# Lent PSUM banks for the first chunks, identity products for the prior state, fewer weight pieces, another end, and an order read from a table

## The chip, the cores and the metric

The kernel runs on one core of a Trainium2 chip. The metric is device time in microseconds (us) of one execution, median of three runs. TensorE (PE) multiplies matrices, VectorE (DVE), ScalarE (ACT) and GpSimd (POOL) do elementwise work, SyncE (SP) issues most transfers. PSUM is the memory that PE writes its products to; SBUF is the other on-chip memory.

## The reference

A linear recurrence over 768 steps feeds two feed-forward layers. Cut to what matters:

```python
# r, k, v, w, a, b: [4, 8, 768, 40]; state: [4, 8, 40, 40]
for t in range(768):
    y[:, :, t] = einsum('bhd,bhde->bhe', r_t, state)
    Sa = einsum('bhde,bhe->bhd', state, a_t)
    state = state * w_t[..., None, :] - einsum('bhd,bhe->bhde', Sa, b_t) + einsum('bhd,bhe->bhde', v_t, k_t)
x = y as [3072, 320]                       # tokens x model
x = (relu(x @ w_in1) ** 2) @ w_out1        # w_in 320x2048, w_out 2048x320
h = x @ w_in2
return (h * cos(h)) @ w_out2               # [3072, 320]
```

The four weight matrices arrive as float64, which the kernel reads as pairs of 32-bit integers and turns into float32 itself.

## The kernel before, in words

**The recurrence** is cut into 12 chunks of 64 steps, and its 32 heads into 16 pairs, worked on in 4 groups of 4 pairs. For each chunk `decay` makes running products of w (`lam`, forwards, and a backward scan) with two scans per group on DVE; the scans need a row that is 1.0 at each head's start and 0.0 elsewhere, which stands in the constants `kc` in SBUF (`K_SC`). Two tensors of a chunk, `cin` and `at`, are multiplied with the decays. A solve by 32x32 blocks follows, and then for each group a short chain: `pq` and `pp` from the state, `px`, `pu`, and last `py`, the products that hold the chunk's outputs and the next state's new part. The prior state's part of the outputs is copied to a tile `sz` and added to `py` afterwards on DVE, and the state `MT` is added likewise. The PSUM tiles of these chains come from a ring named `att` with 3 buffers.

**The weights.** Each of 16 column blocks f of a layer has 704 columns (384 of w_in, 320 of w_out). To convert one, ACT makes `u` and `w` from the integers (clamp), DVE works out the bits with two TENSOR_SCALAR and one SCALAR_TENSOR_TENSOR on `u`, POOL adds, and then ACT copies the high half to `ws` while DVE or POOL subtracts it, so that `ws` holds a high and a low part (`split`). Of layer 1, the first `EARLY` blocks are converted by `first`, each in two parts of 384 and 320 columns; the others in the pieces that `PIECES` lists, mixed into the recurrence. Layer 2's blocks 0 to 7 are converted in pieces as well and written back to memory (`w2f`); blocks 8 to 15 are done whole by `Weights.late`, in tiles `wr`, after the recurrence.

**The feed-forward layers** work on blocks of 512 tokens, one column block f a step: 8 matmuls make `h` from the high and low halves of the input (`xh`, `xl`), the activation is made in halves `gh` and `gl`, and 8 matmuls (`po`, layer 1) or 12 (`pt`, layer 2) apply w_out. `h` and `po0`, `po1`, `po2` have PSUM banks of their own. A block of layer 1 needs the outputs of two chunks.

**What sets the order.** Up to the last chunk all operations are first put in a `Book`, with a kind: recurrence, weights, or layer 1. `Book.arrange` then puts them in order greedily, by rank, costs, `BONUS` and the shifts in `PRIORITY`, and chooses the engine of those that may run on two. The rest (the end of layer 1 with `late` woven in by slots, and all of layer 2) is issued in the order of the code. In the profile, line 1058 is the Book's and line 313 the direct part's.

Of the kernel before, what the change touches and what calls it, by code (L numbers as in the profile page):

```python
# [29 lines left out]
EARLY = 8  # L30
# [10 lines left out]
PIECES = ((0, 256), (256, 128), (384, 160), (544, 160))  # L41
# [8 lines left out]
K_ME, K_MO, K_ID, K_RS, K_ONE, K_LIM, K_QT, K_LOW = 0, 104, 208, 248, 249, 250, 251, 252  # L50
# [83 lines left out]
def f32_of_bits(bits):  # L134
# [14 lines left out]
    {'m': 1287429.0, 'y': 1504832.0, ('w', 0): 338963.0, ('w', 1): 299763.0, 'evict': 3771576.0, 'wait': 0.0, ('w', 2): -2016099},  # L149
    {'m': -914107.0, 'cfg': 166353.0, 'stay': 1197706.0})  # L150
# [168 lines left out]
class Nc:  # L319
# [10 lines left out]
    (('c', 0), 'Ls'): -5,  # L330
    (('c', 0), 'M0d'): -19,
    (('c', 0), 'MT0'): 92,
    (('c', 0), 'MT1'): 50,
    (('c', 0), 'MT2'): 48,
    (('c', 0), 'MT3'): 66,
    (('c', 0), 'Ts0'): -4,
    (('c', 0), 'Ts1'): -6,
    (('c', 0), 'at'): 36,
    (('c', 0), 'cin'): -2,
    (('c', 0), 'ga'): -179,  # L340
    (('c', 0), 'kc'): -2,
    (('c', 0), 'l21'): -192,
    (('c', 0), 'lam0'): 169,
    (('c', 0), 'lam2'): -170,
    (('c', 0), 'lent'): 42,
    (('c', 0), 'pm'): -56,
    (('c', 0), 'pn'): 251,
    (('c', 0), 'pp'): -1,
    (('c', 0), 'pt'): -120,
    (('c', 0), 'pu'): -2,  # L350
    (('c', 0), 'pw'): 1,
    (('c', 0), 'px'): -19,
    (('c', 0), 'py'): -68,
    (('c', 0), 'rv'): 1,
    (('c', 0), 't11'): -5,
    (('c', 0), 'tcomp'): -54,
    (('c', 0), 'tt'): -21,
    (('c', 0), 'ttmp'): 38,
    (('c', 0), 'xsb'): -284,
    (('c', 0), 'yt'): -4,  # L360
    (('c', 1), 'Ls'): 55,
    (('c', 1), 'M0d'): -62,
    (('c', 1), 'MT0'): -6,
    (('c', 1), 'MT1'): -19,
    (('c', 1), 'MT2'): 21,
    (('c', 1), 'MT3'): -14,
    (('c', 1), 'ga'): -121,
    (('c', 1), 'kc'): 81,
    (('c', 1), 'l21'): 37,
    (('c', 1), 'lam1'): -4,  # L370
    (('c', 1), 'lent'): -2,
    (('c', 1), 'mov'): -5,
    (('c', 1), 'pgt'): -17,
    (('c', 1), 'pn'): 123,
    (('c', 1), 'pp'): -93,
    (('c', 1), 'pq'): 38,
    (('c', 1), 'pt'): 7,
    (('c', 1), 'pu'): 84,
    (('c', 1), 'pw'): -22,
    (('c', 1), 'px'): 160,  # L380
    (('c', 1), 'py'): -13,
    (('c', 1), 'rv'): -42,
    (('c', 1), 'sz'): 6,
    (('c', 1), 'tcomp'): -72,
    (('c', 1), 'tt'): -10,
    (('c', 1), 'ttmp'): -347,
    (('c', 1), 'xsb'): 3,
    (('c', 10), 'L'): -21,
    (('c', 10), 'M0d'): 115,
# [12 lines left out]
    (('c', 10), 'pgt'): 100,
    (('c', 10), 'pm'): 2,
    (('c', 10), 'pp'): 11,
    (('c', 10), 'pq'): -2,
    (('c', 10), 'pt'): -28,
    (('c', 10), 'pu'): 87,
    (('c', 10), 'pw'): -22,
    (('c', 10), 'px'): -21,
    (('c', 10), 'py'): 98,  # L410
    (('c', 10), 'rv'): 178,
    (('c', 10), 'sz'): 19,
    (('c', 10), 't11'): -37,
    (('c', 10), 'tcomp'): 43,
    (('c', 10), 'tt'): 2,
    (('c', 10), 'ttmp'): 32,
    (('c', 10), 'xsb'): 32,
    (('c', 10), 'yt'): 123,
    (('c', 11), 'L'): -5,
    (('c', 11), 'Ls'): 156,  # L420
    (('c', 11), 'Tw'): -17,
    (('c', 11), 'at'): -125,
    (('c', 11), 'cin'): 135,
    (('c', 11), 'ga'): -9,
    (('c', 11), 'kc'): -58,
    (('c', 11), 'l21'): -65,
    (('c', 11), 'lam2'): 55,
    (('c', 11), 'mov'): 15,
    (('c', 11), 'pgt'): -37,
    (('c', 11), 'pp'): 51,  # L430
    (('c', 11), 'pq'): -21,
    (('c', 11), 'pt'): -85,
    (('c', 11), 'pu'): -8,
    (('c', 11), 'pw'): 48,
    (('c', 11), 'px'): 43,
    (('c', 11), 'py'): 49,
    (('c', 11), 'rv'): -107,
    (('c', 11), 'sz'): -11,
    (('c', 11), 't11'): -12,
    (('c', 11), 'tcomp'): 10,  # L440
    (('c', 11), 'tt'): -58,
    (('c', 11), 'ttmp'): 162,
    (('c', 11), 'xsb'): -209,
    (('c', 11), 'yt'): 68,
    (('c', 2), 'Ls'): -12,
    (('c', 2), 'M0d'): -46,
    (('c', 2), 'MT0'): -13,
    (('c', 2), 'MT1'): -157,
    (('c', 2), 'MT2'): -87,
    (('c', 2), 'MT3'): -46,  # L450
    (('c', 2), 'Ts0'): 45,
    (('c', 2), 'at'): -1,
    (('c', 2), 'cin'): 7,
    (('c', 2), 'ga'): -67,
    (('c', 2), 'kc'): 224,
    (('c', 2), 'l21'): -156,
    (('c', 2), 'lent'): -3,
    (('c', 2), 'mov'): -7,
    (('c', 2), 'pgt'): 6,
# [297 lines left out]
class Book:  # L757
# [1506 lines left out]
```

## Time and profile before

| | us |
|---|---|
| three runs | 1123.14, 1125.52, 1125.87 (median 1125.52) |
| profiled execution, its own time | 1125.96 |
| its span, first to last instruction | 1124.1 |
| PE busy | 1031.2 (92%) |
| DVE busy | 729.4 (65%) |
| ACT busy | 668.2 (59%) |
| POOL busy | 548.2 (49%) |
| first matmul of a feed-forward layer | 169.3 |
| end of the Book's part, about | 700 |
| layer 2, about | 768 to 1116 |

Around the span lie 1.9 us more. "Busy" is the time in which an engine executed something; a wait is put down to the instruction that was finished last before the waiting one could go (its releaser). In the views of stretches below, the engines stand in the order PE, PEld (PE's weight loads), DVE, ACT, POOL, each with its instructions in brackets, and then the granted clock of TensorE (1.00 is 2.4 GHz, 0.50 is 1.2 GHz), the busy share of the DMA engines and what they moved.

### The profile page before, as it was taken

To read this page: it belongs to the slowest core of one execution; us is meant where nothing else is said; L and a number is where in the kernel's file an instruction comes from. 1 tells how busy PE (TensorE), PEld (TensorE's weight loads), DVE (VectorE), ACT (ScalarE), POOL (GpSimd) and SP (SyncE) were. 2 spreads that over 40 slices of the span, in tenths; PEclk is the share of its full clock that TensorE was granted. 3 is DMA by queue.
4 is the path that set the end of the run, shared out by engine and by line. 5 is a ranking of instruction groups with operands and counts; after the bars stand their busy time and mean duration, and the time that the engine had idled before them with its cause. 6 is when DMAs were issued, how large, how long until landed. Compare 5 with 4: busy or idle time off the path is not lost.

```text
span 1124.1 us, 29832 instructions
## 1 busy us (share of the span) xinstructions
PE 1031.2 (92%) x11778; PEld 860.6 (77%) x11778; DVE 729.4 (65%) x1507; ACT 668.2 (59%) x1397; POOL 548.2 (49%) x939
## 2 busy tenths in 40 slices
PE   3357889996999999999999999899999999999996
PEld 3256677774677777777777788688999999999996
DVE  8878789879786868786866434258953434343432
ACT  5347568775766556665755655676565656565653
POOL 3453427575654846464645521469943333333332
PEclk9996769998899999999999999899999999999999
DMA  9763474747467565756454422541010101010000
GB/s 259 172 177 108 87 161 108 164 112 176 103 161 154 150 138 144 160 137 150 115 122 114 86 56 53 198 155 52 1 52 1 52 1 52 1 52 1 24 1 27
DMA packets 245269, 113.44 MB, mean 101 GB/s; under 512 B 201648, under 2 KB 224528, under 8 KB 244224
## 3 DMA queue, kind: packets, MB, share of 16 engines
q1 hardware_dynamic: 243152, 110.83, 39.9%
q8 instruction: 95, 1.56, 0.6%
q10 hardware_dynamic: 1968, 0.60, 0.2%
q14 instruction: 54, 0.44, 0.1%
HBM read 87.13 MB, written 24.26 MB: 99 GB/s over the span
## 4 chain that ended last, share of the span: by engine, by line
PE 75%; DVE 8%; ACT 5%; DMA 5%; issue 3%; POOL 1%; SPq 1%; ACTq 0%; DVEq 0%; POOLq 0%
PE h L313 18%; PE pt L313 15%; PE h L1058 13%; PE po L1058 12%; PE po L313 3%; PE pu L1058 3%; PE py L1058 3%; PE px L1058 2%; PE pgt L1058 2%; DMA w<-moe 1%; DVE u L1058 1%; PE pq L1058 1%; PE pp L1058 1%; SPq L1058 1%; DVE mov L1058 1%
## 5 line engine op out<-in xcount | busy, mean ns | idle before, releaser
L313 POOL TENSOR_TENSOR gl<-g,gh 128x512 fp32r<-128x512 f32 x113 | 148.0, 1310 | 219.1 <-ACT gh L313 172.7
L313 PE MATMUL h<-xh,ws 128*128 128x512 f32 x560 | 183.9, 393 | 3.0 <-ACT g L313 3.0
L1058 POOL TENSOR_TENSOR ttmp<-tcomp,L 128x126 f32<-128x126 f32 (+22 forms) x279 | 116.8, 418 | 76.7 <-DMA tt<-Tw 19.7
L1058 PE MATMUL h<-xh,ws 128*128 128x512 f32 x400 | 139.3, 410 | 5.0 <-ACT ws L1058 3.3
L313 PE MATMUL h<-xl,ws 128*128 128x512 f32 x336 | 132.7, 395 | 0.1
L313 DVE SCALAR_TENSOR_TENSOR g<-n,h 128x512 f32<-128x512 int32 x96 | 66.0, 687 | 102.4 <-ACT n L313 101.5
L1058 POOL TENSOR_TENSOR tcomp<-tcomp,ttmp 128x126 f32<-128x126 f32 (+22 forms) x279 | 122.2, 438 | 19.8
L1058 PE MATMUL po<-gh,ws 128*128 128x512 f32 x385 | 123.1, 407 | 9.3 <-ACT ws L1058 6.3
L313 ACT ACTIVATE n<-h 128x512 int32<-128x512 f32 x96 | 57.2, 596 | 120.3 <-PE h L313 120.3
L313 PE MATMUL pt<-ws,gh 128*128 128x320 f32 x768 | 128.1, 308 | 0.5 <-DVE g L313 0.4
L313 PEld LDWEIGHTS pt<-ws,gh 128*128 128x128 f32 x768 | 119.9, 188 | 8.3 <-DVE g L313 0.6
L313 PEld LDWEIGHTS h<-xh,ws 128*128 128x128 f32 x560 | 105.8, 189 | 24.0 <-ACT g L313 3.5
L313 DVE TENSOR_TENSOR g<-g,h 128x512 f32<-128x512 f32 x96 | 65.8, 686 | 71.0 <-ACT g L313 71.0
L1058 POOL TENSOR_TENSOR u<-u,w 128x160 int32<-128x160 int32 (+4 forms) x80 | 56.8, 713 | 86.0 <-DVE u L1058 60.8
L1058 PEld LDWEIGHTS h<-xh,ws 128*128 128x128 f32 x400 | 75.5, 190 | 27.7 <-ACT ws L1058 4.3
L1058 PE MATMUL h<-xl,ws 128*128 128x512 f32 x240 | 96.2, 404 | 0.0
L1058 PEld LDWEIGHTS po<-gh,ws 128*128 128x128 f32 x385 | 69.8, 189 | 27.7 <-ACT ws L1058 6.7
L313 ACT ACTIVATE g<-g,kc 128x512 f32<-128x512 f32 x96 | 69.7, 726 | 26.2 <-DVE g L313 24.6
L1058 PE MATMUL po<-gl,ws 128*128 128x512 f32 x231 | 79.9, 403 | 0.3 <-DVE gl L1058 0.3
L1058 PE MATMUL pgt<-at,cin 40*64 40x104 f32 x1536 | 58.3, 286 | 23.2 <-DVE cin L1058 12.6
L1058 DVE TENSOR_TENSOR mov<-pu,kc 64x416 f32<-64x416 f32 (+1 forms) x96 | 49.8, 519 | 42.8 <-PE pu L1058 39.1
L1058 PEld LDWEIGHTS pgt<-at,cin 40*64 40x64 f32 x1536 | 45.9, 153 | 37.1 <-issue 17.5
(144 smaller groups left out, 2149.4 us busy)
## 6 DMA issues: line engine op xcount, KB each, us to landing
rv<-rv SPq DMA_DIRECT2D x48, 256.0 KB
w<-moe SPq DMA_DIRECT2D x16, 704.0 KB
cin<-cin SPq DMA_DIRECT2D x8, 896.0 KB
Ls<-ga SPq DMA_DIRECT2D x48, 128.0 KB
w<-moe SPq DMA_DIRECT2D x32, 160.0 KB
L<-Ls SPq DMA_DIRECT2D x36, 128.0 KB
w<-moe SPq DMA_DIRECT2D x16, 256.0 KB
lent<-cin SPq DMA_DIRECT2D x9, 448.0 KB
```

Source lines behind the costliest of these rows:

```text
L313: return fn(*[real(z) for z in args], **{k: real(z) for k, z in kw.items()})
L1058: fn(*[real(z) for z in args], **{k: real(z) for k, z in kw.items()})
```

## The change

It has six parts.

1. `LENT = 3`: for chunks 0 to 2 the scans read their pattern from a PSUM bank (`po2`, lent until layer 1 needs it), filled once; the later chunks read `kc` as before.
2. For chunks 1 and 2 the prior state is no longer copied and added: 8 small matmuls with an identity (`py<-mov,kc`) put it into the `py` bank, and the products add to it there. These `py` stand in banks lent from `po0`, `po1`, `h` and `h3`; so do chunk 0's. For chunks 3 to 11 the additions are written in place in `py`, and the two multiplications by the decay read `py`.
3. `EARLY` goes from 8 to 7, `first` converts a block whole (704 columns, in the tile that block f+1 will have), and the pieces are 3 a block instead of 4.
4. In `late` the clamp, bits and add of a block move ten slots later; its load stays.
5. The last step's activation is done in two halves of 256 columns, its `gl` on DVE, the last matmuls go by pairs of output tiles, and every second output is copied by DVE and sent from ACT's queue.
6. The Book's order, with the choice of engine, is read from a table of 4358 entries instead of being worked out. The printed order of the changed kernel is that table's.

```diff
-EARLY = 8
+EARLY = 7
...
+LENT = 3
+PIECES = ((0, 256), (256, 256), (512, 192))
...
+ORDER = (
+    18, 6, 2, 10, 8, 68, 70, 72, 12, 74, 4, 76, 78, 32, 101, 666, 42, 50, 38, 36, 40, 48, 664, 706,
...
     def flush(self):
-        self.arrange()
+        if len(self.ops) == ORDERED:
+            self.recorded()
+        else:
+            self.arrange()
         self.emit()
+    def recorded(self):
+        self.order = []
+        for z in ORDER:
+            o = self.ops[z // 2]
+            if o.ways:
+                o.eng = list(o.ways)[z % 2]
+                o.cost, o.calls = o.ways[o.eng]
+            self.order.append(o)
...
+                if last < NF:
+                    u = st[k] = m.p1.tile([128, SW], F32R, tag=f"w{f + 1}", name="u0").bitcast(F32)[:, 0:n]
...
-            for t, c0, n in ((5, 0, 384), (6, 384, DM)):
+            for k, (c0, n) in enumerate(((0, NW),) if last < NF else ((0, 384), (384, DM))):
...
-            return [(0, load), (8, clamp), (12, lambda: self.bits(st["w"], st["u"])),
-                    (17, lambda: self.add(st["w"], st["u"], st["u"]))]
+            return [(0, load), (18, clamp), (22, lambda: self.bits(st["w"], st["u"])),
+                    (27, lambda: self.add(st["w"], st["u"], st["u"]))]
...
+        self.ones = bank("po2", "ones")[0:104, 0:455]
+        vec.memset(self.ones, 0.0)
+        vec.memset(self.ones[:, 64:195:65], 1.0)
...
-            sz = self.p2.tile([128, 4, 64], F32, tag="sz", name="sz", bufs=2)
-            self.copy(sz[0:104], qv[0:104])
+            if c < LENT:
+                yv = self.bank(("po0", "po1", "h", "h3")[g], "py")[:, 0:416].rearrange("p (a b) -> p a b", b=104)
+                for j in range(4):
+                    nc.tensor.matmul(yv[64:104, j], kc[64:104, K_ID:K_ID + 40], mov[64:104, j], start=j == 0, stop=False)
+                    nc.tensor.matmul(yv[0:64, j], kc[0:40, K_ID:K_ID + 64], mov[0:40, 4 + j], start=j == 0, stop=False)
...
-            if c:
-                self.vec.tensor_tensor(mt[0:104], yv[0:104, :, 64:104], mt[0:104], op=ALU.add)
-            self.vec.tensor_tensor(mt[0:104], mt[0:104] if c else yv[0:104, :, 64:104],
+            if old:
+                self.vec.tensor_tensor(yv[0:104, :, 64:104], yv[0:104, :, 64:104], mt[0:104], op=ALU.add)
+            self.vec.tensor_tensor(mt[0:104], yv[0:104, :, 64:104],
...
-        nc.gpsimd.tensor_tensor(gl, g, gh, op=ALU.subtract)
+        for s in cols:
+            nc.scalar.activation(gh[:, s], g[:, s], AF.Copy)
+            (self.vec if len(cols) > 1 else nc.gpsimd).tensor_tensor(gl[:, s], g[:, s], gh[:, s], op=ALU.subtract)
...
+        (self.nc.scalar if last and j % 2 else self.nc.sync).dma_start(self.out[j, bass.ds(128 * blk, 128)], o)
...
+                last = e == len(steps) - 1
+                seq = [z for js in ((0, 1), (2, 3)) if last for z in (
+                    *((j, gh, ws) for j in js for ws in (0, 1)), *((j, gl, 0) for j in js))]
```

How the change moves instructions, at the three places that matter below. First PE, where the first feed-forward matmuls stand in the Book's order. Before, they came in the middle of chunk 2's chains (`pq`, `pp`, `px` are steps of a group's chain):

```order
L1058 MATMUL pq<-rv,M0d 64x64
L1058 MATMUL h<-xh,ws 128x512
L1058 MATMUL h<-xl,ws 128x512
L1058 MATMUL h<-xh,ws 128x512
L1058 MATMUL h<-xl,ws 128x512
L1058 MATMUL h<-xh,ws 128x512 x4
L1058 MATMUL pp<-rv 64x64 x8
L1058 MATMUL px<-mov,ga 64x104 x8
```

Now they stand behind chunk 2's last `py`, among chunk 3's first products (`pm` and `pgt` are a chunk's first):

```order
L837 MATMUL py<-mov,ga 40x104
L837 MATMUL py<-mov,ga 64x104
L837 MATMUL pm<-kc,MT_123 40x40 x8
L837 MATMUL pgt<-at,cin 64x104 x16
L837 MATMUL h<-xh,ws 128x512
L837 MATMUL h<-xl,ws 128x512
L837 MATMUL h<-xh,ws 128x512 x3
L837 MATMUL h<-xl,ws 128x512
```

Counted in the two orders, 1274 matmuls stood ahead of the first `h`, and 1450 do now, the 64 identity products among them; ahead of the first `h` that uses block 15, 238 feed-forward matmuls stood, and 224 do now.

Second ACT, at the start of the direct part, right behind `xh` of a new block. A step's `g`, `g`, `gh` are its relu, square and high half; `wr<-w` and `w<-w` are the clamp of a `late` weight block. Before:

```order
L313 ACTIVATE xh<-xf 128x512 x3
L313 ACTIVATE g<-h 128x512
L313 ACTIVATE g<-g 128x512
L313 ACTIVATE gh<-g 128x512
L313 ACTIVATE wr<-w_10645 128x704
L313 ACTIVATE w_10645<-w_10645 128x704
L313 ACTIVATE g<-h 128x512
```

Now two more steps stand ahead of the clamp:

```order
L314 ACTIVATE gh<-g 128x512
L314 ACTIVATE g<-h 128x512
L314 ACTIVATE g<-g 128x512
L314 ACTIVATE gh<-g 128x512
L314 ACTIVATE g<-h_10523 128x512
L314 ACTIVATE g<-g 128x512
L314 ACTIVATE gh<-g 128x512
L314 ACTIVATE wr<-w_10486 128x704
```

Third PE at the very end: `pt` are the four output tiles of the last block, each with two `gh` products and one `gl` product in the last step. Before, all `gh` products came first:

```order
L313 MATMUL pt_15824<-ws,gh 128x320 x2
L313 MATMUL pt_15825<-ws,gh 128x320 x2
L313 MATMUL pt_15826<-ws,gh 128x320 x2
L313 MATMUL pt_15827<-ws,gh 128x320 x2
L313 MATMUL pt_15824<-ws,gl 128x320
L313 MATMUL pt_15825<-ws,gl 128x320
```

Now two tiles are finished before the other two begin:

```order
L314 MATMUL pt_15670<-ws,gh 128x320 x2
L314 MATMUL pt_15671<-ws,gh 128x320 x2
L314 MATMUL pt_15670<-ws,gl 128x320
L314 MATMUL pt_15671<-ws,gl 128x320
L314 MATMUL pt_15672<-ws,gh 128x320 x2
L314 MATMUL pt_15673<-ws,gh 128x320 x2
```

Other counts from the two orders, on DVE ahead of the last `ws` of block 15: TENSOR_SCALAR on `u` 96 before and 70 now, SCALAR_TENSOR_TENSOR on `u` 48 and 35, subtractions into `ws` 46 and 40, products `cin` (104x512) 25 and 16, `at<-lent,lam` 4 and 1, copies `xsb` 4 and 9, and nineteen more of the smaller copies and `gl` that ACT or POOL did before. What `cin` and `at` lose on DVE, POOL does.

## Rows read from the trace of the kernel before

**Rows 1.** Windows: stretch, length, busy us (count) per engine, granted clock, DMA, GB/s.

```profile
...
0.00:284.69 284.69, 206.52 (x3871) 168.71 (x3871) 238.80 (x587) 171.60 (x433) 141.64 (x289) 0.88 0.63 153
150.00:170.00 20.00, 16.52 (x311) 14.41 (x306) 16.25 (x42) 13.72 (x32) 7.16 (x16) 0.55 0.94 214
169.32:284.69 115.37, 101.81 (x1330) 77.26 (x1327) 99.24 (x248) 79.52 (x208) 75.77 (x152) 0.95 0.59 140
298.00:700.00 402.00, 400.04 (x5525) 316.39 (x5525) 279.12 (x616) 241.78 (x537) 205.09 (x465) 1.00 0.54 122
...
```

**Rows 2.** Timeline of PE: start, us, engine, line, operation, count.

```profile
...
169.32 0.50 PE L1058 MATMUL h<-xh,ws 128*128 128x512 f32 x1
...
191.38 0.93 PE L1058 MATMUL py<-mov,ga 128*40 128x104 f32 x16
...
284.69 0.79 PE L1058 MATMUL h<-xh,ws 128*128 128x512 f32 x1
...
```

**Rows 3.** Waits, 170 to 298 us: waiter, releaser, total us, times, longest.

```profile
...
ACT ws L1058 <- POOL u L1058: 22.2, 11, 4.8
...
PE po L1058 <- ACT ws L1058: 6.3, 1, 6.3
...
```

**Rows 4.** Groups on DVE to 298 us: busy us, mean ns, idle before.

```profile
...
L1058 DVE TENSOR_SCALAR u<-u 128x160 f32<-128x160 f32 (+6 forms) x96 | 34.6, 364 | 4.6 <-ACT u L1058 3.3
L1058 DVE SCALAR_TENSOR_TENSOR u<-w,u 128x160 int32<-128x160 int32 (+4 forms) x48 | 20.9, 441 | 1.1
...
L1058 DVE TENSOR_TENSOR ws<-u,ws 128x256 fp32r<-128x256 f32 (+4 forms) x47 | 16.5, 369 | 5.5 <-ACT ws L1058 5.4
...
L1058 DVE TENSOR_TENSOR cin<-cin 104x512 f32<-104x512 f32 x14 | 9.0, 681 | 0.0
...
L1058 DVE TENSOR_TENSOR sz<-py,sz 104x256 f32<-104x256 f32 x12 | 4.9, 417 | 1.7 <-PE py L1058 1.7
...
L1058 DVE TENSOR_TENSOR MT<-py,MT 104x160 f32<-104x160 f32 x12 | 3.7, 314 | 0.1
...
```

**Rows 5.** Groups by form on DVE, 700 to 765 us.

```profile
...
L313 DVE SCALAR_TENSOR_TENSOR wr<-w,wr 128x704 int32<-128x704 int32 x8 | 8.1, 1015 | 0.3
L313 DVE TENSOR_SCALAR wr<-wr 128x704 f32<-128x704 f32 x8 | 7.4, 920 | 30.2 <-ACT wr L313 30.2
L313 DVE TENSOR_SCALAR wr<-wr 128x704 int32<-128x704 int32 x8 | 5.6, 704 | 0.3
...
```

**Rows 6.** Groups on POOL, 0 to 298 us.

```profile
...
L1058 POOL TENSOR_TENSOR cin<-cin 104x512 f32<-104x512 f32 x2 | 2.4, 1177 | 0.0
...
```

**Rows 7.** Timeline around the start of the direct part: SP, ACT, PE.

```profile
...
702.91 1.27 SPq L313 DMA_DIRECT2D w<-moe  x2
...
709.31 0.83 ACT L313 ACTIVATE wr<-w 128x704 f32<-128x704 f32 x1 [6.51 <-DMA w<-moe]
...
706.40 1.30 PE L313 MATMUL po<-gh,ws 128*128 128x512 f32 x5
707.53 0.84 PE L313 MATMUL po<-gl,ws 128*128 128x512 f32 x3
711.41 0.80 PE L313 MATMUL h<-xh,ws 128*128 128x512 f32 x1 [3.04 <-ACT g L313]
...
718.18 0.39 PE L313 MATMUL h<-xh,ws 128*128 128x512 f32 x1
...
```

**Rows 8.** Timeline of DVE at the start of layer 2.

```profile
...
763.25 3.85 DVE L313 TENSOR_TENSOR xl<-xf,xh 128x512 fp32r<-128x512 f32 x3 [0.71 <-ACT xh L313]
...
```

**Rows 9.** Timeline at the end: ACT, POOL, PE, SP.

```profile
...
1112.72 0.63 ACT L313 ACTIVATE gh<-g 128x512 fp32r<-128x512 f32 x1 [0.76 <-DVE g L313]
...
1113.48 1.30 POOL L313 TENSOR_TENSOR gl<-g,gh 128x512 fp32r<-128x512 f32 x1 [1.11 <-ACT gh L313]
...
1114.84 0.85 PE L313 MATMUL pt<-ws,gl 128*128 128x320 f32 x4
...
1115.75 2.92 SPq L313 DMA_DIRECT2D out<-o  x4
...
```

More of the change, by code (lines that the diff above doesn't have):

```diff
@@ L901, in flush @@
     def flush(self):
-        self.arrange()
+        if len(self.ops) == ORDERED:
+            self.recorded()
+        else:
+            self.arrange()
         self.emit()
+    def recorded(self):
[6 more added lines that the diff above has]
+            self.order.append(o)
+        kept = {o.k for o in self.order}
+        self.rest = [o for o in self.ops if o.k not in kept]
     def arrange(self):
@@ L1370, in backward @@
             s = slice(260 * q, 260 * q + 260)
[L1371 removed]
+            self.vec.tensor_tensor_scan(wf[:, s][:, ::-1], wi[:, s][:, ::-1],
+                                        (self.ones[:, 195:455] if lent else one)[:, ::-1], 1.0, op0=ALU.mult, op1=ALU.add)
         def inverse(q):
[L1374 removed]
+            self.vec.reciprocal(self.ones[:, 259:455:65] if lent else one[:, 64::65], lam[:, 4 * q:4 * q + 4, 64])
         def again(q):
[L1377 to L1378 removed]
+            if q == 3 and not lent:
+                self.nc.gpsimd.memset(one[:, 64::65], 1.0)
         todo = [(fn, q) for q in range(4) for fn in (forward, inverse, backward, again)]
@@ L1687, in state @@
         yield
-        py = self.att.tile([128, 512], F32, tag="att", name="py")
-        yv = py[:, 0:416].rearrange("p (a b) -> p a b", b=104)
+        old = c and c >= LENT
+        if c == 0 or old:
+            py = self.att.tile([128, 512], F32, tag="att", name="py") if old else self.bank(("po0", "po1", "h", "h3")[g], "py")
+            yv = py[:, 0:416].rearrange("p (a b) -> p a b", b=104)
+        fresh = c == 0 or bool(old)
         for j in range(4):
-            nc.tensor.matmul(yv[64:104, j], ga[:, 8 + h4 + j, 64:104], mov[:, j], start=True, stop=True)
+            nc.tensor.matmul(yv[64:104, j], ga[:, 8 + h4 + j, 64:104], mov[:, j], start=fresh, stop=fresh or j == 3)
             b0 = 104 * (h4 + j) + 64
-            nc.tensor.matmul(yv[0:64, j], gf[:, b0:b0 + 64], mov[:, 4 + j], start=True, stop=True)
+            nc.tensor.matmul(yv[0:64, j], gf[:, b0:b0 + 64], mov[:, 4 + j], start=fresh, stop=fresh or j == 3)
         mt = self.MT[g]
@@ L1959, in pipeline @@
                 gs[q] = []
-                act = self.act(layer, h, gs[q])
+                act = self.act(layer, h, gs[q], 1 + (q == len(steps) - 1))
                 for _ in act:
```

504 lines of the change are left out of this document (45 added, 459 removed), and 181 rows, old and new, of the table ORDER.

## The prediction, made before the changed kernel ran

> **What bounds the kernel now.** I read the windows first, because the bound changes along the span. Between 298 and 700 us PE is busy 400.0 of 402 us at clock 1.00 [rows 1]: there PE is the limit, and only fewer or shorter matmuls would help. Up to the first use of weight block 15, at 284.69 [rows 2], it is different: PE is busy 206.5 of 284.7 us, DVE 238.8, ACT 171.6, POOL 141.6 [rows 1]. DVE is the fullest engine there. The waits then say who holds PE up: PE's `po` waited 6.3 us for ACT's `ws`, and ACT's `ws` 22.2 us in all for POOL's `u` [rows 3], which is made from DVE's bits. So the early part is a chain DVE, POOL, ACT, PE for converted weights, with DVE the engine that has least room. Once all blocks are converted PE never waits long again. A shift of the moment at which block 15 is there therefore shifts the whole rest, less what PE then has more to do.
>
> Two small places remain: the start of the direct part, where PE idles 3.04 us and then works at half its pace [rows 7], and the end, where nothing overlaps [rows 9].
>
> The sum is made against the profiled execution's own 1125.96 us (span 1124.1 and 1.86 around it); the median of the runs is 1125.52, 0.44 less. About 0.3%, 3.4 us, is what a measurement of this kernel can tell from no change.
>
> **The early part, DVE's work ahead of block 15.** With counts from the two orders:
>
> Weight pieces. A TENSOR_SCALAR on `u` takes 364 ns on 235 columns (704 in three pieces, on average), and 812 ns, the mean of the 920 and 704, on 704 [rows 4, 5]; that is 0.95 ns a column and 0.14 us for each instruction. In the same way SCALAR_TENSOR_TENSOR, 441 and 1015 ns, gives 0.15 us. 26 and 13 fewer instructions: -3.6 and -2.0. One more piece of 256 columns stands ahead now: +0.8. Together -4.8. The rows of 704 columns were taken beside other traffic, so what one instruction costs may be more (twice as much gives -10.4); with no cost per instruction it would be +0.8.
>
> Sums of chunks 1 and 2: 8 groups lose `sz<-py,sz` (417 ns) and `MT<-py,MT` (314 ns) [rows 4]: -5.9. What replaces them is 64 matmuls on PE, which are counted below.
>
> Products `cin` and `at`: twelve of 512 columns go to POOL, at 0.681 on DVE [rows 4]: -8.2. POOL pays 12 at about 1.18 [rows 6], 14.1 us, and was busy half the time.
>
> Subtractions into `ws`: six fewer at 0.369 [rows 4]: -2.2.
>
> Copies that ACT or POOL did: five `xsb` of 416 columns at about 0.6, an estimate between the 417 ns of 256 columns and the 681 of 512 [rows 4], and nineteen mostly smaller ones at 0.417: +10.9. The pattern in PSUM instead of SBUF I cost at nothing; the same 32 scans stay on DVE.
>
> Sum -10.2, priced so; nothing hides any of it as long as DVE is fullest. If DVE's idle time stays (284.7 - 238.8 = 45.9 us up to block 15), block 15's first `h` goes from 284.7 to 274.5.
>
> **Can PE follow?** The first `h` moves behind chunk 2, since its banks are lent: 176 more matmuls ahead of it. At 150 to 170 us, at clock 0.55, PE put through 311 in 20 us [rows 1], 0.064 each, so 11.3 us later: 169.3 becomes about 181. From there to block 15 PE was busy 101.8 us [rows 1]; it now has 14 feed-forward matmuls less (0.226 us each: five in the 1.13 from 706.40 to 707.53 [rows 7]; -3.2) and those 176 less (-11): 88. So PE is ready at 269, before 274.5; DVE still decides, with 5 us to spare. The 64 identity products lie ahead of 181, where PE idled 64.6 of 169.3 us (78.2 idle up to 284.69, 13.6 of it after 169.32, [rows 1]); without that cover they cost 64 x 0.064 = 4 us. The 14 matmuls must be done later, when PE is the limit: +3.2.
>
> Early part: -10.2 + 3.2 = **-7.0**.
>
> **A point against it**: the twelve products on POOL, beside more copies on DVE. At 763.25 us three `xl` took 3.85 us on DVE, while POOL was splitting weights [rows 8]; at the 681 ns of a DVE product of the same size [rows 4] three take 2.0. The Trainium skill (SBUF — State Buffer, Who interferes with whom) says that a DVE instruction with two SBUF inputs contends with a GpSimd instruction that reads SBUF, for the whole of the instruction; the row agrees, and by that rule the moved products would give up to 14.1 us back. DVE's largest early group, TENSOR_SCALAR on `u` with 34.6 us [rows 4], reads one tensor, so I leave it to a rival.
>
> **Chunks 3 to 11.** The additions in `py` are as many as before, and the two multiplications now read PSUM. `py` is held for those two as well, about 0.73 us in each of 36 groups (the 417 and 314 ns rows): at most 26 us if PE waited for a bank every time, nothing if a feed-forward matmul fills the gap. PE idles 2 of 402 us in this stretch [rows 1], and feed-forward matmuls are always at hand, so **0**.
>
> **The start of the direct part.** SP issues the load of the first `late` block at 702.91, ACT's clamp waits 6.51 us for it and starts at 709.31, and the steps queued behind it on ACT (relu, square, `gh`) hold PE: from the end of the last `po` at 708.37 to the `h` at 718.18 lie 9.8 us, in which 16 matmuls ran that take 16 x 0.226 = 3.6 at full pace [rows 7]. That is 6.2 us lost, idle and slow pace together. Two more steps (3.6 us each) stand ahead of the clamp now, so it comes to the front about when the load has landed, and holds nothing up: -6.1, a little kept back. Later the last block's bits (2.64 us, [rows 5]) fall between the `ws` casts at the start of layer 2, ahead of `xl` [rows 8]. `xl` was followed at once by PE's `h`, so 0 to 2.6 us later; I take 1. Together **-5.1**, between -6.5 and 0.
>
> **The end.** `gl` on POOL took 1.30 us, to 1114.78, and PE's last products waited for it [rows 9]. In halves, three steps ahead of `gh` save about 0.3 us each and `gh` itself (0.63) 0.3: PE starts about 1.2 earlier than 1113.4. Its 12 products still take 2.3 us, with the second halves ready in time. Four sends took 2.92 us in one queue [rows 9]; two queues save about one send, 0.6 of it exposed: **-1.8**, between -2.4 and 0.
>
> Sum: 1125.96 - 7.0 - 5.1 - 1.8 = 1112.06, **1112**. Its own range is 1104 to 1119.
>
> **Rivals.**
>
> B. Chunk 2 does not end earlier: its last `py` started at 191.4 us, and the next chunk's `pgt` right behind [rows 2]; if latency from group to group sets that, and not DVE's load, the first `h` comes at 194 and block 15 at 194 + 88 = 282: -2.7 + 3.2 - 6.9 = -6.4: **1120**. For it: PE, ACT and POOL all have gaps in this stretch. Against it: DVE was busy 16.25 of 20 us at 150 to 170 [rows 1]. Chance 0.15.
>
> C. The first `h` does not slip, since chunk 2 is done sooner with less on DVE, and DVE's idle time shrinks too: block 15 at 169 + 88 = 257, -27.7 + 3.2 - 6.9: **1095**. For it: with DVE fullest at 150 to 170 us [rows 1], less work on it moves chunk 2 forwards as well. Against it: the 176 matmuls more. Chance 0.10.
>
> D, the other side. Nothing but small matmuls now runs on PE before the first `h`. Before, `h` matmuls from 169.3 on were followed by clock 1.00 (0.95 on average up to 284.7, against 0.55 at 150 to 170 [rows 1]). If the stretch from 170 to 192 is now run at half clock as well, it takes up to 22 us longer and the first `h` comes at 214: block 15 at 302, +17.3 + 3.2 - 6.9 = +13.6, **1140**. It decides from a first `h` at 204 on (204 + 88 = 292 is 3.4 us more than the rest gives back). The Trainium skill (TensorE: Matmul & The Clock Gate, Part 1) has it that the throttled state is the default and activity releases it, and the low clock of these stretches agrees. Against it: DVE, not PE, is fullest there. Chance 0.08.
>
> E. `py` held longer does stop PE in the middle: half of the 26 us gives **1125**, all 1138. Chance 0.08, half of it slower by over 0.3%.
>
> F. DVE stands still while POOL does the twelve products, as it seemed to at 763.25 [rows 8]: 14.1 back, +3.9 + 3.2 - 6.9 = +0.2, **1126**. Chance 0.06.
>
> My forecast has 0.53. Faster by over 0.3%: it, B and C, 0.78. Within: half of E, most of F, 0.08. Slower: D, the other half of E, some of F, 0.14. The range 1094 to 1125 holds the forecast, B, C and the lower half of E, about 0.8.
>
> **What the changed profile would show.** The first `h` at about 181 (B: 194, C: 169, D: over 204); the first `h` of block 15 at about 274; PE 298 to 700 still busy over 99%, with no wait for `py`'s readers (E); clamps behind three steps with no wait for the load, and no half clock near 710; `xl` of layer 2 a microsecond or two later; last send about 1.8 us nearer to the last step's `h`. I am wrong if the clock before the first `h` is lower than now, if the early gain comes without a shift of block 15, or if POOL's early instructions and DVE's two-input ones are both longer than in the rows.

## The result, and the profile after

The changed kernel took 1112.32 us (median of six runs, 1110.28 to 1115.02); the kernel before, in runs on the same chips, 1126.07. The ratio is 0.988, with a 95% interval of 0.9862 to 0.9898: 11 to 16 us less. The profiled execution has a span of 1109.9 us against 1124.1.

Where the 14.2 us of the spans come from is read best on PE, since every feed-forward matmul of the one kernel has its partner in the other. The table gives the start of certain ones, counted in the trace (PE's matmuls of 512 or 320 columns, in order of time): the first; number 1271, by which all small matmuls of the recurrence are done in both; 1321, behind the start of the direct part; 1521, just ahead of layer 2's first `xl`; 1561, in layer 2. "Last h" is the end of the last `h`.

```
            first h   no.1271  no.1321  no.1521  no.1561   last h     span
before        169.3    702.3    720.0    765.3    774.8   1109.7   1124.1
after         186.8    691.8    704.8    750.1    762.7   1097.6   1109.9
difference    +17.5    -10.5    -15.2    -15.2    -12.1    -12.1    -14.2
```

So: the Book's part gives 10.5, the start of the direct part 4.7 more, layer 2's start takes 3.1 back, and the end gives 2.1. The forecast had 7.0, 6.1, 1 and 1.8. The sum was met, the parts less well.

These are differences of two single traces. The same Book ran in two more kernels on either side (table of the experiments): number 1271 came at 702.3, 704.5 and 706.2 with the Book of before, at 690.8, 691.8 and 692.1 with the changed one. So the Book's part is worth 10.5 by these two traces and 12.7 by the means of three, and a difference of 2 us there can't be read from one pair of traces.

**The Book's part.** Windows of the kernel before, cut at its first `h`, at 298 us (just behind the last `ws` of block 15) and near the end of the recurrence's small matmuls, at 697.4 (columns as in [rows 1]):

```profile
...
0.00:169.32 169.32, 104.71 (x2545) 91.45 (x2545) 139.56 (x341) 92.08 (x226) 65.87 (x138) 0.84 0.65 161
169.32:298.00 128.68, 114.35 (x1517) 86.84 (x1515) 107.78 (x267) 89.27 (x231) 81.87 (x168) 0.95 0.59 138
298.00:697.40 399.40, 397.44 (x5513) 314.51 (x5513) 278.94 (x615) 240.88 (x534) 203.79 (x464) 1.00 0.54 122
...
```

The same of the changed kernel, cut at its own first `h`, at the last `ws` of block 15, and at 687.0, where as many small matmuls are left:

```profile
...
0.00:186.82 186.82, 121.92 (x2896) 106.39 (x2897) 151.00 (x360) 93.94 (x226) 93.99 (x174) 0.84 0.65 156
186.82:287.50 100.68, 98.57 (x1250) 77.42 (x1252) 81.52 (x192) 73.49 (x175) 67.32 (x130) 1.00 0.68 154
287.50:687.00 399.50, 396.78 (x5565) 315.02 (x5558) 278.40 (x603) 222.11 (x479) 245.98 (x487) 1.00 0.55 124
...
```

PE is busy for the same time in both, 616.5 and 617.3 us. Its idle time is what differs: 64.6 and 64.9 us up to the first `h`, although that comes 17.5 us later now; 14.3 and 2.1 in the middle stretch; 2.0 and 2.7 in the last. The gain lies in the middle stretch, between the first `h` and block 15: 12.2 us less of idle time, of which 1.8 are lost again elsewhere. Before, PE waited there for `ws` ([rows 3]; 11.0 us with the smaller waits); now none of its waits there names `ws`. The granted clock fits: 0.95 there before, 1.00 now, and 0.84 up to the first `h` in both.

The timeline of PE around the first `h`, and around the first `h` of block 15 (284.69 before [rows 2]):

```profile
...
183.59 1.38 PE L837 MATMUL py<-mov,ga 128*40 128x104 f32 x16 [0.38 <-DVE mov L837]
...
186.82 0.47 PE L837 MATMUL h<-xh,ws 128*128 128x512 f32 x1 [0.69 <-DVE yt L837]
...
273.83 0.57 PE L837 MATMUL pp<-rv 40*64 40x64 f32 x14
274.33 0.50 PE L837 MATMUL h<-xh,ws 128*128 128x512 f32 x1
...
```

Block 15's `h` comes at 274.33, 10.4 us sooner, directly behind small matmuls and without any wait. Chunk 2's last `py` starts at 183.59, where it started at 191.38 [rows 2]. ACT's copies of the first piece of block 15, before and in the changed kernel, say when the weights were there:

```profile
...
284.22 0.42 ACT L1058 ACTIVATE ws<-u 128x256 fp32r<-128x256 f32 x1 [1.77 <-POOL u L1058]
...
272.44 0.40 ACT L837 ACTIVATE ws<-u 128x256 fp32r<-128x256 f32 x1
...
```

They are there 11.8 us sooner. Before, PE's `h` followed at once (284.64, then 284.69); now PE comes 1.5 us after them (272.84, then 274.33).

DVE's groups up to 290 us in the changed kernel:

```profile
...
L837 DVE TENSOR_SCALAR u<-u 128x256 f32<-128x256 f32 (+5 forms) x70 | 26.8, 394 | 2.1 <-ACT u L837 1.2
...
L837 DVE SCALAR_TENSOR_TENSOR u<-w,u 128x256 int32<-128x256 int32 (+2 forms) x35 | 18.6, 537 | 0.5
...
```

The weights' bits take 26.8 + 18.6 = 45.4 us instead of 34.6 + 20.9 = 55.5 [rows 4]: 10.1 less, at the far end of what the prediction gave as the bound. That this is what brought block 15's weights forward is likely but not shown, since no run undoes the pieces alone.

**The direct part.** ACT's timeline shows a clamp that waits for nothing (`gh` of a step, then `wr` and `w`, then the next step):

```profile
...
706.35 0.63 ACT L314 ACTIVATE gh<-g 128x512 fp32r<-128x512 f32 x1
706.89 0.82 ACT L314 ACTIVATE wr<-w 128x704 f32<-128x704 f32 x1
707.61 0.84 ACT L314 ACTIVATE w<-w 128x704 int32<-128x704 uint32 x1
708.97 0.60 ACT L314 ACTIVATE g<-h 128x512 f32<-128x512 f32 x1 [0.52 <-PE h L314]
...
```

PE's waits from there into layer 2:

```profile
...
700.11 1.21 PE L314 MATMUL po<-gh,ws 128*128 128x512 f32 x4 [0.39 <-ACT o L314]
701.92 0.50 PE L314 MATMUL po<-gh,ws 128*128 128x512 f32 x1 [0.60 <-DVE o L314]
...
751.66 0.50 PE L314 MATMUL h<-xl,ws 128*128 128x512 f32 x1 [1.14 <-DVE xl L314]
...
752.95 0.50 PE L314 MATMUL h<-xl,ws 128*128 128x512 f32 x1 [0.31 <-DVE xl L314]
...
755.06 0.50 PE L314 MATMUL h<-xl,ws 128*128 128x512 f32 x1 [1.15 <-DVE xl L314]
...
```

The 3.04 us and the slow matmuls of [rows 7] are gone; 0.99 us of waits for `o` are there in their place. The three waits for `xl` are new, and DVE shows why: the last block's bits (745.91 to 748.4) and a block's casts stand ahead of `xl`, and `xl` itself takes 4.34 us for three, against 3.85 before [rows 8].

```profile
...
745.91 1.66 DVE L314 TENSOR_SCALAR wr<-wr 128x704 f32<-128x704 f32 x2 [0.92 <-ACT wr L314]
747.60 0.89 DVE L314 SCALAR_TENSOR_TENSOR wr<-w,wr 128x704 int32<-128x704 int32 x1
...
749.87 0.87 DVE L314 CAST ws<-wr 128x320 fp32r<-128x320 f32 x1
750.67 4.34 DVE L314 TENSOR_TENSOR xl<-xf,xh 128x512 fp32r<-128x512 f32 x3
...
```

**The end.** PE, ACT's sends and SP's in the changed kernel:

```profile
...
1100.61 0.85 PE L314 MATMUL pt<-ws,gl 128*128 128x320 f32 x4
1101.29 0.75 PE L314 MATMUL pt<-ws,gh 128*128 128x320 f32 x4
...
1102.90 0.37 ACTq L314 DMA_DIRECT2D out<-o  x1
...
1103.78 0.37 ACTq L314 DMA_DIRECT2D out<-o  x1
...
1102.69 1.48 SPq L314 DMA_DIRECT2D out<-o  x2
...
```

### The profile page after: what moved, and what is told of

It reads as the page before. It is cut to its first block, busy times and chain, and to the rows that moved or that the text cites. A ratio compares the mean times of both kernels' runs of the same rounds, so it can differ in the third digit from the quotient of the medians.

```text
span 1109.9 us, 29826 instructions
## 1 busy us (share of the span) xinstructions
PE 1029.5 (93%) x11906; PEld 864.6 (78%) x11906; DVE 718.6 (65%) x1444; ACT 635.0 (57%) x1287; POOL 603.8 (54%) x959
## 4 chain that ended last, share of the span: by engine, by line
PE 76%; DVE 8%; ACT 5%; DMA 4%; issue 3%; POOL 2%; SPq 1%; ACTq 0%; POOLq 0%; DVEq 0%
PE h L314 17%; PE pt L314 15%; PE po L837 12%; PE h L837 11%; PE py L837 4%; PE pu L837 3%; PE px L837 3%; PE pgt L837 3%; PE po L314 2%; DMA w<-moe 2%; PE pq L837 2%; DVE mov L837 2%; PE pp L837 2%; POOL u L837 1%; PE pt L837 1%
## 5 line engine op out<-in xcount | busy, mean ns | idle before, releaser
L314 PE MATMUL h<-xh,ws 128*128 128x512 f32 x560 | 182.6, 391 | 0.0
L837 POOL TENSOR_TENSOR tcomp<-tcomp,ttmp 128x126 f32<-128x126 f32 (+22 forms) x279 | 126.4, 453 | 20.5
L837 PE MATMUL h<-xh,ws 128*128 128x512 f32 x400 | 136.7, 402 | 0.7 <-DVE yt L837 0.7
L314 PE MATMUL h<-xl,ws 128*128 128x512 f32 x336 | 132.2, 393 | 2.6 <-DVE xl L314 2.6
L314 DVE SCALAR_TENSOR_TENSOR g<-n,h 128x512 f32<-128x512 int32 (+1 forms) x97 | 66.1, 682 | 103.5 <-ACT n L314 102.9
L314 DVE TENSOR_TENSOR g<-g,h 128x512 f32<-128x512 f32 (+1 forms) x97 | 66.0, 681 | 71.1 <-ACT g L314 71.1
L837 POOL TENSOR_TENSOR u<-u,w 128x256 int32<-128x256 int32 (+2 forms) x58 | 58.6, 1012 | 77.9 <-DVE u L837 24.2
L837 PE MATMUL h<-xl,ws 128*128 128x512 f32 x240 | 94.1, 398 | 0.0
L314 ACT ACTIVATE g<-g,kc 128x512 f32<-128x512 f32 (+1 forms) x97 | 69.9, 721 | 27.0 <-DVE g L314 25.8
L837 ACT ACTIVATE g<-h 128x512 f32<-128x512 f32 x79 | 47.0, 595 | 64.3 <-PE h L837 37.3
L314 PEld LDWEIGHTS h<-xl,ws 128*128 128x128 f32 x336 | 63.0, 188 | 13.4 <-DVE xl L314 3.9
L314 PE MATMUL pt<-ws,gl 128*128 128x320 f32 x384 | 72.2, 309 | 0.0
```

Source lines behind the costliest of these rows:

```text
L314: return fn(*[real(z) for z in args], **{k: real(z) for k, z in kw.items()})
L837: fn(*[real(z) for z in args], **{k: real(z) for k, z in kw.items()})
```

## The experiments

Times are medians; the ratio is to the kernel before on the same chip. The first `h` comes at 186.8, 185.6, 186.5 and 189.3 in the four kernels below in which nothing ahead of it differs (after, after_late_13, after_late_12, after_ws_dve), so a shift of it by less than 3 us says nothing. No run undoes part 1 (the lent pattern) or part 3 (the pieces) alone.

```
kernel               first h  no.1271  no.1321  no.1521  no.1561   last h     span   ratio (95% interval)
after                  186.8    691.8    704.8    750.1    762.7   1097.6   1109.9   0.9880 (0.9862 to 0.9898)
after_prod_dve         194.7    700.0    712.9    758.2    770.4   1105.4   1117.5   0.9938 (0.9919 to 0.9956)
after_sums_dve         194.4    703.1    716.1    761.4    773.7   1108.7   1120.8   0.9954 (0.9935 to 0.9974)
after_ident_twice      194.4    702.0    714.9    760.3    772.5   1107.5   1120.9   0.9929 (0.9904 to 0.9955)
after_ident_pair       189.0    693.5    706.4    751.8    764.1   1099.0   1112.3   0.9881 (0.9839 to 0.9923)
after_ws_dve           189.3    698.2    711.1    756.5    768.7   1103.7   1115.7   0.9915 (0.9885 to 0.9944)
after_greedy           209.1    736.7    749.6    794.9    807.2   1142.1   1154.6   1.0245 (1.0203 to 1.0288)
before_plain           167.0    737.1    752.9    798.2    807.6   1142.6   1157.1   1.0335 (1.0299 to 1.0372)
before_late_slots      168.4    706.2    719.1    764.4    776.7   1111.7   1126.1   0.9993 (0.9972 to 1.0015)
before_end             170.2    704.5    721.4    766.7    776.2   1111.1   1124.5   1.0000 (0.9980 to 1.0020)
after_late_13          185.6    690.8    704.8    750.2    759.7   1094.7   1107.7   0.9849 (0.9816 to 0.9881)
after_late_12_pool     192.2    699.7    712.6    758.0    767.4   1102.3   1114.3   0.9891 (0.9849 to 0.9932)
after_late_12          186.5    692.1    705.1    750.4    759.7   1094.7   1107.9   0.9871 (0.9841 to 0.9900)
```

### Does DVE's work ahead of the first h decide? after_prod_dve

```diff
-                o.eng = list(o.ways)[z % 2]
+                o.eng = list(o.ways)[z % 2 ^ (o.k in MOVED)]
```

`MOVED` holds the fifteen products; the order stays.

> The changed kernel, with the fifteen products cin and at that POOL makes before 160 us put on DVE, at their places in the order. About 0.69 us each, 10.4 us more on DVE ahead of the first h. If DVE's load decides when the first h comes (prediction's step, carried to the first h), the first h moves from 186.8 to 195 or more and the time rises by 8 to 10 us, to about 1121. If these products are hidden in DVE's idle time, under 3 us. If POOL's reads held DVE up (rival F), the time falls.

Measured 1120.53 us. The first `h`:

```profile
...
194.74 0.79 PE L838 MATMUL h<-xh,ws 128*128 128x512 f32 x1
...
```

7.9 us later than in the changed kernel, and the last `h` is 7.8 later; by the ratios the loss is 0.0058 of 1126, 6.5 us. DVE's work ahead of the first `h` (10.4 us) is paid for here at some three quarters of its length by the first `h`, at 0.63 by the ratios, and a shift of the first `h` is passed on whole. These fifteen products do not cost more on POOL than they save on DVE: rival F is out for them.

The traces show why, and what part 1 of the change has to do with it. Below, POOL's product and DVE's scan run at the same time, in the kernel before (pattern in `kc`, SBUF) and in the changed kernel (pattern in `ones`, PSUM):

```profile
...
17.80 1.18 POOL L1058 TENSOR_TENSOR at<-lent,lam 104x512 f32<-104x512 f32 x1 [10.92 <-PE pgt L1058]
18.47 1.07 DVE L1058 TENSOR_TENSOR_SCAN lam<-lent,kc 104x259 f32<-104x259 f32 x1
...
18.67 1.19 POOL L837 TENSOR_TENSOR cin<-lent,cin 104x512 f32<-104x512 f32 x1
18.62 0.68 DVE L837 TENSOR_TENSOR_SCAN lam<-lent,ones 104x259 f32<-104x259 f32 x1
...
```

A scan takes 0.65 to 0.70 us when POOL is idle, wherever its pattern stands. Of the 39 DVE instructions that overlap with the fifteen products in the changed kernel, 35 read PSUM, and none of these scans took over 0.70; three products with both inputs in SBUF took 1.42, 0.92 and 0.75 instead of 0.68. The Trainium skill (SBUF — State Buffer, Who interferes with whom) states the rule: a DVE instruction with two SBUF inputs contends with a GpSimd instruction that reads SBUF. These rows agree. So F's mechanism exists, and the changed kernel mostly keeps out of its way; what the lent pattern is worth in time no run shows.

### DVE's work behind the first h: after_ws_dve

The same edit, with nine subtractions.

> The changed kernel, with the nine subtractions into ws that POOL makes between the first h and block 15 put on DVE: about 3.3 us more on DVE there. If DVE's load still decides when block 15 comes, 3 us more, about 1115. If PE is full from its first h on and the weights are only just ahead of it, nothing that can be measured, and block 15's first h stays within 1 us of 274.3.

Measured 1116.7. The first `h` came 2.5 us later by chance (nothing ahead of it was changed), 1.9 us were added by number 201 (up to 270 us), and another 1.5 between numbers 401 and 601. The interval reaches into that of the changed kernel. So it is not shown whether DVE work in this stretch is free; a small cost, up to half of the 3.3 us, is likelier than none. Block 15's first `h` came at 278.4, 89.1 us behind the first `h` instead of 87.5. PE has no wait for block 15 left, but the weights are only 1.5 us ahead of it in the changed kernel.

### Identity products or sums: after_ident_twice, after_ident_pair, after_sums_dve

The first two change the calls of the eight recorded operations, where the table's order is read:

```diff
+            if o.eng == "PE" and o.calls[0][1][0].base.kw["name"] == "py" and o.calls[0][1][1].base.kw["name"] == "kc":
+                o.calls = o.calls + [(fn, args, {**kw, "start": False}) for fn, args, kw in o.calls]
```

for the first, and `o.calls = o.calls[:2]` under the same condition for the second.

> The changed kernel, with every identity product issued twice (the prior state of chunks 1 and 2 is counted twice, so its outputs are not the reference's). 64 products more ahead of the first h, 128 records of 0.05 to 0.06 us. If PE lies on the path to the first h, it comes 6 to 7 us later, and the time is 1118 to 1119. If they hide behind DVE, as the prediction has it for the first 64, less than 2 us.

> The changed kernel with one pair's identity products kept in each group and six of eight left out (so the prior state of three of four pairs is missing in chunks 1 and 2, and the outputs are not the reference's). 96 records less ahead of the first h. If the products are on the path, as twice as many cost 7.6 us, the first h comes about 5 us earlier, and the time falls by as much. If they are hidden, under 1.5 us, and the 7.6 of the other run came from what stood behind them alone.

The first `h`, with the products twice:

```profile
...
194.45 0.79 PE L839 MATMUL h<-xh,ws 128*128 128x512 f32 x1
...
```

and with a quarter of them:

```profile
...
189.03 0.79 PE L839 MATMUL h<-xh,ws 128*128 128x512 f32 x1
...
```

Twice costs 7.6 us at the first `h` (5.5 by the ratios); three quarters left out gain nothing (the time is 1113.25). The cost is not a straight line: at least those 48 of the 64 products lie in PE's idle time, as the prediction had it, and 64 more do not.

The third puts the sums back, in the recorded order:

```diff
-            if c < LENT:
-                yv = self.bank(("po0", "po1", "h", "h3")[g], "py")[:, 0:416].rearrange("p (a b) -> p a b", b=104)
-                for j in range(4):
-                    nc.tensor.matmul(yv[64:104, j], kc[64:104, K_ID:K_ID + 40], mov[64:104, j], start=j == 0, stop=False)
...
+            if c < LENT:
+                sz = self.lentL[c][:, 256 + 256 * g:512 + 256 * g].rearrange("p (a b) -> p a b", b=64)
...
-        old = c and c >= LENT
+        old = c > 0
```

The copies go to a free part of a lent weight tile; in the order they stand behind the other readers of `pq`, the additions ahead of the multiplications by the decay.

> The changed kernel in its own order, but chunks 1 and 2 add the prior state on DVE as before: the 64 identity products are gone, eight copies (ACT) and sixteen additions (DVE) are put in their places, and the lent banks stay lent. DVE has 5.9 us more ahead of the first h, PE 128 records (about 7 us) less. If only DVE's load decides, the first h comes 4 to 6 us later. If the products lie as much on the path as the run that issued them twice suggests (7.6 us), the two cancel: within 2 us of 186.8, and the identity products gained nothing.

Measured 1121.97. The first `h`:

```profile
...
194.44 0.79 PE L655 MATMUL h<-xh,ws 128*128 128x512 f32 x1
...
```

The expectation that the two cancel was wrong: with the sums the kernel is 0.0074 of 1126, 8.3 us, slower than with the identity products (11 by the spans). That is more than the 5.9 us of DVE's additions. The copies, and the place of the new operations in an order made without them, may be the rest; they were not separated.

### Order or operations: after_greedy, before_plain

```diff
-ORDERED = 4358
+ORDERED = -1
```

in the changed kernel; in the kernel before an empty `PRIORITY` and the changed kernel's `BONUS`.

> The changed kernel with its order worked out by the greedy ordering (its own round bonuses, no shifts) instead of read from the table. If the early gain is that of less work on DVE, most of the 10 us stays, and the time is 1112 to 1118. If the gain is that of the table, it is lost: over 1125.

> The kernel before, ordered greedily with the bonuses of the changed kernel and without the table of shifts. It stands to the changed kernel under greedy order as one set of operations to the other in the same kind of order. If the parts of the change gain by their work, this one is slower than the changed kernel under greedy order by 10 us or more. If the gain is that of the table, the two are within 5 us, and both slower than the kernel before.

The first kernel falls under its second case (the gain is lost), by far more than that case had; the second lies at the border of its two cases. Greedily ordered, the changed kernel takes 1155.8 and the one before 1164.03. The shifts, with the bonuses they were made for, were worth 0.0335 of the time to the kernel before, 38 us; the table is worth 0.0365, 41 us, to the changed one. Between the two greedy ones lie 0.9%, 10 us, clear of both intervals, of which some 4 belong to the direct part and the end (418.1 us behind number 1271 in the changed kernel, 421.8 before). Whether the rest lies in the Book is open: up to number 1271 the profiles are equal (736.7 and 737.1), but the profiled execution of the one was the slowest of its four runs (1156.38), that of the other the fastest (1158.96). So under a greedy order the operations gain between nothing and some 6 us in the Book, where 10.5 or more were gained with the table; and moved back within the table's order, products or sums lose 6.5 and 8.3 us. Operations and an order made for them go together here.

### The late weights: before_late_slots, after_late_13, after_late_12_pool, after_late_12

The first is the kernel before with the diff's slots 18, 22 and 27 alone.

> The kernel before, with the ten slots' shift of the late weights alone. By the prediction -5 us (6 lost at 708 to 718 come back, 1 given away at layer 2's xl). By the two traces -1.6: the start gives about 4.7 back, and xl costs 3.1. The h that waits for xl should be idle three times, together 2.5 to 3 us.

Measured: no difference (0.9993). From number 1271 to 1321 it gains 17.7 - 12.9 = 4.8 us on the kernel before, and from 1521 to 1561 it loses 2.8. Its waits on PE from 700 to 790 us:

```profile
...
PE h L313 <- DVE xl L313: 2.3, 3, 1.2
PE po L313 <- DVE o L313: 0.6, 1, 0.6
PE po L313 <- ACT o L313: 0.4, 1, 0.4
...
```

That is the trade seen in the changed kernel, by this one edit alone.

The second kernel, in the changed one's code:

```diff
-            return [(0, load), (18, clamp), (22, lambda: self.bits(st["w"], st["u"])),
-                    (27, lambda: self.add(st["w"], st["u"], st["u"]))]
+            return [(0, load), (15, clamp), (19, lambda: self.bits(st["w"], st["u"])),
+                    (24, lambda: self.add(st["w"], st["u"], st["u"]))]
-        return self.stages([job(f) for f in range(LATE, NF)], 14)
+        return self.stages([job(f) for f in range(LATE, NF)], 13)
```

> The changed kernel, with the late weights' slots at 15, 19 and 24, one block every 13 slots instead of 14: the first clamp still comes behind its load, and the last block's bits come as early against layer 2 as they did in the kernel before. If xl waits for those bits alone, the 3.1 us at the start of layer 2 come back: 1109. If the bits only move against POOL's and DVE's other work at that place, or the load is late again, 0 to 1 us.

The third and fourth have the old 18, 22 and 27 with a period of 12; the third also has nine products in `MOVED`, from DVE to POOL.

> The changed kernel with the late weights every 12 slots (first clamp at 18 as it was), and with nine more products cin and at, of chunks 3 and 4, on POOL instead of DVE. Late part: the 3.1 us at layer 2's start come back without the 1 us that slots 15, 19, 24 lost at 696 to 705: -3 against the changed kernel. Early part: 6.2 us less on DVE ahead of the first h; at the 7.9 per 10.4 that the run the other way showed, -4.7; but a product takes 1.18 on POOL instead of 0.69, and if POOL's chain of conversions is then late, 0 or a loss. Together 1105 to 1109.

> The changed kernel with one thing changed: a late weight block every 12 slots instead of 14. The first clamp stays where the change put it, and the last block's bits come 14 slots earlier. By the run before, the 3.1 us that PE waits for xl at the start of layer 2 go, and nothing is lost at 696 to 705: 3 us less than the changed kernel, a ratio of about 0.985 to the kernel before. If that run's late part was helped by its later early part, 1 us or less.

With slots 15, 19, 24 and one block every 13, PE's `pt` part starts 3.0 us sooner (759.7), with 1.0 lost from number 1271 to 1321. With only the period changed to 12, the same 759.7, and nothing lost there: 12.9 us from number 1271 to 1321 as in the changed kernel. The bits are now done before `xl` becomes ready, and DVE goes on to it at once:

```profile
...
747.31 1.02 DVE L314 CAST ws<-wr 128x320 fp32r<-128x320 f32 x1
748.30 3.74 DVE L314 TENSOR_TENSOR xl<-xf,xh 128x512 fp32r<-128x512 f32 x3
...
```

Both spans are 2 us shorter than the changed kernel's, and their medians, 1109.46 and 1110.29, lower; their intervals overlap with its own, so by time alone this is not shown, by the traces it is (twice -3.0 at number 1561). The nine products on POOL lost instead of gaining: the first `h` came 5.4 us later than in the changed kernel, 5.7 later than in the fourth kernel, which has the same late weights. The trace shows that DVE was not relieved. Up to the first `h` it ran nine instructions less, and yet was busy for 153.1 us instead of 151.3: the instructions that are the same in both took 7.5 us longer together, most of it beside the moved products. At one place, POOL and DVE with the products moved, and then DVE in the fourth kernel:

```profile
...
156.25 4.82 POOL L838 TENSOR_TENSOR cin<-cin 104x512 f32<-104x512 f32 x4 [17.25 <-DMA cin<-cin]
157.53 1.19 DVE L838 TENSOR_SCALAR u<-u 128x256 f32<-128x256 f32 x1
158.75 2.61 DVE L838 COPY ga<-at 40x512 f32<-40x512 f32 x2
...
151.79 0.29 DVE L837 TENSOR_SCALAR u<-u 128x256 f32<-128x256 f32 x1
152.11 0.86 DVE L837 COPY ga<-at 40x512 f32<-40x512 f32 x2
...
```

Each of these took about as long as a product beside it (1.17 to 1.36 us). That is rival F's mechanism, for products at another place; that it makes up all of the 5.7 us is not shown.

### The end: before_end

The kernel before with the halves, the pairs of tiles, and the copies and sends of the diff alone.

> The kernel before, with the new end alone. By the prediction -1.8, by the traces -2.1 (from the end of the last h to the end of the span 14.4 before, 12.3 after). If the second queue's send costs what the halves save, 0.

Measured 1126.16, ratio 1.000: nothing that can be told by time. In its profile the last products begin right behind the ones of the step before:

```profile
...
1112.73 1.34 PE L313 MATMUL pt<-ws,gh 128*128 128x320 f32 x8
1113.90 0.78 PE L313 MATMUL pt<-ws,gl 128*128 128x320 f32 x4
1114.52 0.75 PE L313 MATMUL pt<-ws,gh 128*128 128x320 f32 x4
...
```

3.4 us after the last `h`, against 3.7 before; and from the last `pt` to the end of the span lie 8.1 us, against 8.4 before, 6.7 in the changed kernel, and 7.7 and 7.9 in the two late versions. The traces taken together do show a gain: from the end of the last `h` to the end of the span lie 14.4 to 14.5 us in the three kernels of the table with the old end, 12.0 to 13.4 in the eleven with the new one. The end is worth 1 to 2.5 us, less than the interval of before_end (0.2% on either side, 2.3 us) can tell from nothing.

## Why the prediction was right, point by point

**The sum** (1112 forecast, 1112.32 measured) was right, and so was the main reason: PE no longer waits for block 15, whose first `h` came at 274.33, forecast 274.5. The steps were less right than that, and several of them met their numbers by errors that cancel.

**"DVE still decides, with 5 us to spare"** failed. The step had PE ready at 269 and the weights at 274.5; measured were the weights at 272.84 and PE at 274.33. PE has been full since its first `h` (2.1 us of idle time in 100), and what counts is when that `h` comes, 87.5 us earlier. DVE's load moves it (fifteen products, 7.9 us), but so does PE's (64 products twice, 7.6). That the 88 of the prediction was met is luck: the step took 176 matmuls out of the stretch, but the 64 identity products among them had never been in it. What moved out of it is 112 matmuls, 224 records in the trace (1088 small ones before, 864 now), and at 0.05 us each they make the 11 us that the step had.

**"The first `h` at about 181"** failed by 6 us (186.82). The step set 176 matmuls, counted in the order, against a pace of records in the trace. A small matmul of this kernel stands as two records there (the 64 identity products are 128, 2896 - 2544 = 352 for 176). At 0.064 for each record the step would have given 192; 17.5 us for 352 records is 0.05 each.

**The early sum** was mis-sized: -7.0 forecast, -10.5 measured. Block 15's `h` moved by 10.4, where 10.2 were forecast; the term that failed is the +3.2 for the fourteen matmuls that are done later. From block 15's first `h` to number 1271 lie 417.6 us before and 417.5 now, although the fourteen are in it. Why they cost nothing there is not settled; of the 13 us behind that `h`, PE idled 0.8 at clock 0.90 before, 0.03 at 1.00 now.

The -10.2 itself was met by two errors. Up to the last `ws` of block 15 DVE is busy for 232.5 us instead of 247.3 (sums of the windows), 14.8 less; and its idle time, which was to stay as it was, grew by 4.3. The bits gained 10.1, where 4.8 were set: the step priced instructions of 704 columns by rows of the late part (920, 704 and 1015 ns), and early in the changed kernel the same instructions are shorter (groups by form up to 290 us):

```profile
...
L837 DVE SCALAR_TENSOR_TENSOR u<-w,u 128x704 int32<-128x704 int32 x7 | 5.9, 881 | 0.0
...
L837 DVE TENSOR_SCALAR u<-u 128x704 f32<-128x704 f32 x7 | 3.9, 568 | 0.0
L837 DVE TENSOR_SCALAR u<-u 128x704 int32<-128x704 int32 x7 | 3.9, 565 | 0.1
...
```

The six subtractions fewer gave 0.3 instead of 2.2 (16.5 and 16.2 us in all), since one takes longer now. The identity products lay under other work, as forecast; what the sums alone would have cost was not separated from the copies.

**Chunks 3 to 11** at nothing: right. PE idles 2.7 us from 287.5 to 687, and its waits for `py`'s readers or writers are small (rows of the waits from 298 to 700 us):

```profile
...
PE py L837 <- ACT M0d L837: 1.0, 1, 1.0
...
PE py L837 <- DVE mov L837: 0.2, 1, 0.2
...
```

Rival E is out.

**The start of the direct part**: the mechanism was right, the size -4.7 instead of -6.1, and the price at layer 2's `xl` 3.1 instead of 1 (the bound was 2.6). Together -1.6 where -5.1 was forecast. This error made up for the early part's.

**The end**: -2.1 in the spans, -1.8 forecast, but not as forecast. PE could not start 1.2 us earlier, since the products of the step before kept it busy (1100.61 to 1101.46 in the changed kernel, 1113.9 to 1114.68 in before_end); 0.0 to 0.3 came of it. In the changed kernel 0.4 us of the gain lie between the last `h` and the end of the last `pt` (6.0 before, 5.6 now), and 1.7 behind it, in the copies and sends; this last part differs by over 1 us from one profile to another.

**The rivals.** B had chunk 2 end no earlier and the first `h` at 194; chunk 2's last `py` started 7.8 us earlier. D had the first `h` over 204. Up to it the clock was 0.84 as before, but between the old place of the first `h` and the new one, 169.3 to 186.8, it was 0.80, where before it was 1.00 (170 to 240 us): D's mechanism is there, far weaker than the half clock that D had. C had the first `h` at 169. A first `h` at 187 stands between the forecast's and B's. Why the greedy order of the changed kernel has it at 209 and ends as early as the other greedy one was not followed up.

F's sign came in part: DVE's two-input instructions are longer than in the rows (`cin` 728 ns instead of 681, `ws` of 256 columns 539 instead of 431), most of POOL's products are not (1.18 us in both). The fifteen products are not the cause for `ws`, which takes 538 in after_prod_dve as well; `cin` takes 702 there.

## What to carry to other kernels

Find the moment from which the bounding engine never waits again, and ask what must be done before it: fifteen products moved off the busy engine ahead of that moment paid here at 0.63 to 0.76 of their length; nine more at another place paid nothing, because the busy engine's own instructions became longer beside them. So look at what the busy engine does while the other one has the moved work. What a move pays behind that moment was not settled. An engine may start its main work later and finish sooner, if what it does first would otherwise have been waited for in between. When a stall is moved out of one place, look at what the moved work stands ahead of at its new place; here two thirds of a 4.7 us gain were lost so, and a shorter period gave them back.

## What the runs showed of the hardware

Small float32 matmuls of this kernel appear as two records each, so counts from an order and counts from a trace are in different units. Scans on DVE (104x259 or 104x260) took 0.65 to 0.70 us in the changed kernel while POOL was idle, with the pattern in PSUM or in SBUF. Beside POOL's work the thirteen with the pattern in PSUM still took 0.67 to 0.70, and those with it in SBUF up to 1.23 there, 1.07 in the kernel before, and 1.63 with nine more products on POOL. The prediction set the pattern's place at nothing. A COPY or TENSOR_SCALAR on DVE with one SBUF input was held up by POOL's products too: 1.19 to 1.30 us instead of 0.29 to 0.43 (rows above).
